# An attention kernel that feeds a mixture of experts: the stage between the two, rebuilt

## The chip, the cores and the metric

The kernel runs on one core of a Trainium2 chip. The metric is the device time of one execution in microseconds (us). The kernel before has a median of 377.03 us over three runs (375.7, 377.03 and 379.55).

## What is computed

The reference has two parts. Attention without softmax, per batch b (8) and head h (8), with 576 rows of 64 numbers:

```python
kv  = einsum('bhsd,bhse->bhde', k, v)
out = einsum('bhsd,bhde->bhse', q, kv)
rms = sqrt(mean(out * out, axis=-1) + 1e-06)
x   = out / rms * g_norm          # then (B,H,S,D) -> (B*S, H*D) = 4608 x 512
```

Then each of the 4608 rows goes to at most one of eight experts:

```python
do_compute = x @ w_skip > 0                 # the other rows stay as they are
logits = xc @ w_gate                        # 8 numbers for each row that is computed
e_idx  = argmax(logits)
gate_w = exp(logits - max)[e_idx] / (sum + 1e-09)
y      = gate_w * (relu(xc @ w1[e_idx]) @ w2[e_idx])    # w1: 512x1024, w2: 1024x512
out    = xc + y
```

## The kernel before

**Attention in units.** The row tiles of attention are worked off as 36 units, numbered n from 0 to 35 (`NU = 36`). A unit is two tiles of 128 rows for half of the heads; two units in a row (u = 0 and 1) make whole rows. The last two units, 34 and 35, take the ninth row of every 64-row group of the last four batches and use small 64x64 products (L504) where the others use 128x128 ones (L496). For a unit, in this order: TensorE turns q (`turn`) and multiplies it with the batch's kv (`values`; its columns also carry 9 more numbers for each head, which add up over the heads to the row's 8 logits and its skip score); ScalarE squares the product (L510); VectorE sums the squares (`squares`, L518); ScalarE takes the root (L525); VectorE inverts it (L532) and multiplies all 584 columns by it (`norm`, L537), which makes `xl`; GpSimd adds up the heads' logits (`finish`, L554 to L562) and multiplies by g_norm (L567), which makes `xb`; SyncE stores `xb` into the output (L602, or L591 for the units of the ninth rows). The product of a unit lies in one of two PSUM buffers `o_ps`, or for units 30 and 33 in `sum_ps`. So the product of unit 35 can start only when `xl` of unit 32 has been read from the buffer.

**The order is written out.** Within `manual_schedule` each engine executes in the order of the program's text. The loop over n (0 to 37) calls the stages of several units, and `at(step, part, job)` hangs further jobs into a step, at its parts "early", "mid", "pe", "dve" and "end".

**From rows to experts.** The rows are ranked in three groups of units (`ends`: 12, 22 and 36 row tiles). For each, `choose` finds the expert of each row on VectorE (six small operations, L614 to L634), `rank` counts on TensorE how many rows of each expert came before (16 small products into the PSUM tile `g_ps`), and `number` makes places of it on VectorE, among them `oha_k`, a table of ones and zeros (L677). `hits` (L690) and `weighed` (L698) make a second table, and `place` (L710) multiplies the two on TensorE, so that each slot of an expert gets its row number. `settle` calls `place` for one part of the row tiles and adds what comes out to `srow` on VectorE (L773).

**Expert 0 starts before attention ends.** Experts are taken in the order of their row counts in the first two groups (22 of the 36 row tiles). From these groups the first 192 slots (`KEPT`) of expert 0 are already known. `early` computes their row numbers and gathers those rows from the output by two indirect DMAs (L863: 128 rows, then 64 rows). `first_in(0)` and `first_in(1)` turn them on TensorE (L801), and ScalarE copies them to `xt_first` (L828, L830). `first_in(0)` also starts the load of expert 0's second weight matrix (`load_second`, L346), which waits for its last transpose. `first_layer_1` computes 2 of the 8 column blocks of layer 1 (`IN = 2`, each 4 products of 192 columns, L814) into a PSUM tile `q_ps`, and ScalarE applies relu (L817). Then attention's pools are closed. Behind them the code at the file's end computes the 6 other blocks (`layer_1`, L1112), the last group's rank and numbers, two calls of `settle`, layer 2 of the 192 rows (`layer_2`, L1124), the row tables (`again_rows`, L1051 on TensorE, and `slot_rows`), and gathers all further rows (L1084). Then `experts` goes through the eight experts. For expert 0, `first_tables` and `again_gates` make the gate weights beside layer 1 of the rest of its rows (148 columns, L1112).

A product of FP32 numbers shows up as two records on TensorE, so 4 products are 8 rows in the trace.

Of the kernel before, what the change touches and what calls it, by code (L numbers as in the profile page):

```python
# [17 lines left out]
def kernel(  # L18
# [148 lines left out]
    def dense(count):  # L167

        for _ in range(count):
            nc.tensor.matmul(out=warm_ps[:, :], lhsT=ones[:, :],  # L170
                             rhs=ones[:, :].unsqueeze(1).to_broadcast([P, 4, P]), start=True, stop=True)
# [311 lines left out]

    def values(n):
        _, b, i, u = units[n]
        qT = qTs.pop(n)

        ps = sum_all if n in THIRDS else \
            ps_o.tile([P, 2, 512], FP32, tag="o", name="o_ps")

        done = turn_8(b, u, ps) if i == 0 else None
        for w in range(2):
            for a in range(2):
                cols = slice(a * KD, (a + 1) * KD)
                if i is not None:
                    nc.tensor.matmul(  # L496
                        out=ps[:, w, 0:2 * PK].rearrange("p (r k) -> p r k", r=2)[:, :, cols],
                        lhsT=qT[:, w, a, :], rhs=kvds[b % KVD][:, u, w, :, cols],
                        start=True, stop=True, skip_group_check=True)
                    continue  # L500
                for hf in range(2):
                    for r in range(2):
                        rows, to = slice(r * 64, (r + 1) * 64), slice(hf * 64, (hf + 1) * 64)
                        nc.tensor.matmul(  # L504
                            out=ps[to, r, w * PK + a * KD:w * PK + (a + 1) * KD],
                            lhsT=qT[rows, w, hf, a * 64:(a + 1) * 64],
                            rhs=kvds[(4 * b + 2 * hf + r) % KVD][rows, u, w, r, cols],
                            start=True, stop=True, skip_group_check=True)
        sq = att_pool.tile([P, 2, 2, 2 * D], FP32, tag="sq", name="sq", bufs=2)
        nc.scalar.activation(out=sq[:, :, :, :], in_=heads(ps, G, G + 2 * D), func=ACT.Square)  # L510
        if done:
            done()
        ops[n] = (ps, sq)
# [14 lines left out]
    def norm(n):  # L528

        nq, b, i, u = units[n]  # L530
        (ps, _), rs = ops.pop(n), rss.pop(n)
        inverse = nc.vector.reciprocal(out=rs[:, :, :], in_=rs[:, :, :])  # L532
        if n < NU - 2:
            scale(n, inverse)
        r4 = rs[:, :, :].unsqueeze(3)
        xl = att_pool.tile([P, 2, 2, PK], FP32, tag="xl", name="xl", bufs=4)
        nc.vector.tensor_tensor(  # L537
            out=xl[:, :, :, :].rearrange("p x y (a k) -> p x (y a) k", a=2),
            in0=ps[:, :, 0:2 * PK].rearrange("p x (h k) -> p x h k", k=KD),
            in1=r4.to_broadcast([P, 2, 4, KD]), op=ALU.mult)  # L540
        return lambda: finish(n, xl)

    def finish(n, xl):
        nq, b, i, u = units[n]
        g = sum(2 * nq >= x for x in ends)
        t0 = 2 * nq - ([0] + ends)[g]
# [9 lines left out]
        if u == 1:  # L556
            del halves[nq]
            nc.gpsimd.tensor_tensor(out=lp[:, 0, :, :, :], in0=lp[:, 0, :, :, :],
                                    in1=lp[:, 1, :, :, :], op=ALU.add)
            both = lp[:, 0, :, :, :] if i is not None else \  # L560
                lp[:, 0, :, :, :].rearrange("p r w g -> p w r g")
            nc.gpsimd.tensor_tensor(out=lgs[g][:, t0:t0 + 2, :], in0=both[:, 0, :, :],  # L562
                                    in1=both[:, 1, :, :], op=ALU.add)
        if u == 0:
# [8 lines left out]
    def scale(n, behind=None):  # L573

        while late:
# [80 lines left out]
    def number(g):  # L656
# [19 lines left out]
        for t in range(0, nt, step):  # L676
            nc.vector.tensor_tensor(out=oha_k[:, t0 + t:t0 + t + step, :],  # L677
                                    in0=row128_i[:, :].unsqueeze(1).to_broadcast([P, step, P]),
                                    in1=lo_i[:, t:t + step].unsqueeze(2).to_broadcast([P, step, P]),
                                    op=ALU.is_equal)  # L680
# [85 lines left out]
    def settle(t0, t1, bv):  # L766
        sp = g_ps[:, GB:GB + 2 * NCOL]
        place(sp, bv, t0, t1 - t0)
        add_pieces(srow[:, :], sp, 2)

# [19 lines left out]
    IN = 2  # L790
# [4 lines left out]
    def first_in(part):  # L795
# [4 lines left out]
        for j in range(DC * m // P):  # L800
            landed = nc.tensor.transpose(out=xp[:, j, :],  # L801
                                         in_=x_of(xg0, off, m)[:, j * P:(j + 1) * P],
                                         identity=ident[:, :])
        turned(xt_first, xp, off, m)
        if part == 0:
            load_second(0, landed)

    def first_layer_1():

        hps = ps_q.tile([P, 512], FP32, tag="q", name="q_ps")  # L810
        for f in range(IN):
            cols = slice(f * KEPT, (f + 1) * KEPT)
            for dc in range(DC):
                nc.tensor.matmul(out=hps[:, cols], lhsT=w_sb[0][0][:, dc, f * P:(f + 1) * P],  # L814
                                 rhs=xt_first[:, dc, :], start=(dc == 0), stop=(dc == DC - 1),
                                 skip_group_check=True)
        at(NU, "early", lambda: nc.scalar.activation(  # L817
            out=ht_first[:, :, :], in_=hps[:, 0:IN * KEPT].rearrange("p (f t) -> p f t", f=IN),
            func=ACT.Relu))
# [20 lines left out]
    NE = ends[LAST - 1]  # L840

    def early():
# [24 lines left out]
        def put():  # L867
            for t in range(NE):
# [76 lines left out]
    now = [0]  # L945
    for part in range(2):
        at(NU - 3 + 2 * part, "early", lambda part=part: first_in(part))
    at(NU - 1, "end", first_layer_1)

    PACE = (2, 4)  # L950
    for n in range(NU + 2):
# [17 lines left out]
        if n == NU:  # L969
            ohc = hits(0, NE, colid_i, gat_pool, NE)  # L970
            drain(choose(LAST))
            scale(NU, chosen[-1])
            first_bv = weighed(ohc, 0, NE, row_k, 2, gat_pool, NE)
# [17 lines left out]
    with tc.tile_pool(name="wpool_b", bufs=1, reuse_waits="tile") as wpool_b, \  # L991
# [375 lines left out]
        def experts(pieces, widths, srcs, xt, ht, yps0, tables, group):  # L1367

            for r in range(E):
# [17 lines left out]
                if r == 0:  # L1387
# [6 lines left out]
                    enter(more[0:1])  # L1394
# [4 lines left out]
                    enter(more[1:])  # L1399
# [69 lines left out]
        layer_1(0, xt_first, ht0, slice(0, KEPT), range(IN, 5))  # L1469
        rank(LAST)  # L1470
        drain(number(LAST))
        layer_1(0, xt_first, ht0, slice(0, KEPT), range(5, FC))
        settle(0, NE, first_bv)
        last_bv = columns(NE, NT - NE, colid_i, row_k, 2, gat_pool, NE)
        y, y_more = [layer_2(0, ht_of, piece, None, range(IN)) for piece in first]
        settle(NE, NT, last_bv)
        layer_2(0, ht_of, first[0], y, range(IN, 3))
        arows = slot_pool.tile([P, NRES], I32, tag="arows", name="arows")
        asrc = slot_pool.tile([P, NRES], I32, tag="asrc", name="asrc")
        again_rows(arows, asrc, range(0, SOON))  # L1480
        rows, src = slot_rows(slice(0, NCOL), slot_pool, "")
        layer_2(0, ht_of, first[0], y, range(3, 4))
        again_rows(arows, asrc, range(SOON, len(runs)))
        layer_2(0, ht_of, first[0], y, range(4, FC))
        for r in range(3):
            gather_all(r, plan, src, asrc)
        gates()
        layer_2(0, ht_of, first[1], y_more, range(IN, 5))
        for piece in plan[0]:
            landed = expert_in(xg0, xt0, piece)  # L1490
        yps0 = [y, layer_2(0, ht_of, first[1], y_more, range(5, FC))]
# [74 lines left out]
```

## Time and profile before

| | us |
|---|---|
| median of three runs | 377.03 (375.7 to 379.55) |
| the profiled execution, its time | 378.6 |
| the profiled execution, its span | 376.7 |
| TensorE matmul busy | 362.9 (96% of the span) |
| VectorE busy | 244.3 (65%) |
| ScalarE busy | 142.9 (38%) |
| GpSimd busy | 122.7 (33%) |
| mean granted TensorE clock | 0.992 |
| products of the last attention unit (n = 35) start | 116.05 |
| layer 1 on the first 192 rows starts | 117.23 |
| layer 1 on expert 0's other rows starts | 144.27 |

A span is the time from the first to the last instruction of the profiled execution; its own time is 1.9 us longer. PE is TensorE, PEld its weight loads, DVE VectorE, ACT ScalarE, POOL GpSimd, SP SyncE. "L537" is line 537 of the kernel before. The granted clock is the share of TensorE's full clock that the chip allowed in a stretch.

### The profile page before, as it was taken

The page shows a single profiled execution, that of the slowest core. Times are in us where ns is not written, and L with a number is a line of the kernel's source. Part 1 is how long each engine was busy: PE and PEld are TensorE (multiplying, and loading weights), DVE is VectorE, ACT ScalarE, POOL GpSimd, SP SyncE. Part 2 cuts the span into 40 slices and gives each one's busy share as a digit, 9 for nine tenths or more (in the row PEclk, how much of TensorE's full clock was granted, in tenths as well). Part 3 has the DMA queues.
Part 4 walks back from the last instruction along what each step waited for, and adds up shares of the span by engine and source line. Part 5 has one row for each costly group of instructions (what it writes and reads, how often), then busy time and mean ns, then how long its engine had stood idle before and what let it go on. Part 6 is the DMA issues. An engine that isn't in the chain of part 4 may idle for free.

```text
span 376.7 us, 9624 instructions
## 1 busy us (share of the span) xinstructions
PE 362.9 (96%) x3848; PEld 314.8 (84%) x3848; DVE 244.3 (65%) x626; ACT 142.9 (38%) x383; POOL 122.7 (33%) x195
## 2 busy tenths in 40 slices
PE   8899999999988999999999999999999999999994
PEld 4687897898977948779979987988998998998983
DVE  3355367767787763566766675876876776878831
ACT  2466576666773212214402430430440430431420
POOL 7035467655668435323013302202302302102003
PEclk9999999999998999999999999999999999999998
DMA  8999999996487718967427362671762762700001
GB/s 289 395 391 391 401 405 396 405 384 206 132 302 213 232 39 281 392 237 252 168 98 222 114 225 76 239 244 46 284 197 72 274 209 80 269 3 28 30 1 53
DMA packets 32039, 81.70 MB, mean 217 GB/s; under 512 B 2474, under 2 KB 2482, under 8 KB 31988
## 3 DMA queue, kind: packets, MB, share of 16 engines
q1 hardware_dynamic: 28176, 69.47, 52.0%
q0 software_dynamic: 3792, 11.53, 9.2%
q8 instruction: 32, 0.52, 0.6%
q14 instruction: 19, 0.16, 0.1%
q10 hardware_dynamic: 20, 0.02, 0.0%
HBM read 66.80 MB, written 14.48 MB: 216 GB/s over the span
## 4 chain that ended last, share of the span: by engine, by line
PE 82%; issue 6%; DMA 3%; ACT 3%; DVE 3%; POOL 2%; SPq 0%; POOLq 0%; DVEq 0%; ACTq 0%
PE bank L1192 44%; PE bank L1124 9%; PE o_ps L496 6%; PE sum_ps L379 4%; PE bank L1112 4%; PE q_ps L460 3%; PE g_ps L393 2%; DMA v<-in_v_dram 2%; PE bank L1093 2%; PE q_ps L814 1%; DMA xg<-out_dram,src 1%; DVE rs L518 1%; DVE xl L537 1%; ACT sq L510 1%; PE g_ps L411 1%
## 5 line engine op out<-in xcount | busy, mean ns | idle before, releaser
L1202 ACT COPY p<-bank 128x128 f32<-128x128 f32 (+6 forms) x70 | 20.8, 297 | 99.2 <-PE bank L1192 88.5
L1192 PE MATMUL bank<-xt,w 128*128 128x128 f32 (+5 forms) x336 | 55.4, 288 | 0.0
L567 POOL TENSOR_TENSOR xb<-xl,g_b 128x512 f32<-128x512 f32 x36 | 43.5, 1211 | 32.5 <-DVE rs L532 30.6
L1323 POOL DMA_INDIRECT out_dram<-xg,rows x14 | 14.4, 1027 | 120.8 <-DVE xg L1320 117.6
L1192 PEld LDWEIGHTS bank<-xt,w 128*128 128x128 f32 x336 | 47.0, 190 | 1.9 <-DVE bank L1196 1.4
L1196 DVE TENSOR_TENSOR bank<-bank,p 128x128 f32<-128x128 f32 (+6 forms) x70 | 23.6, 337 | 30.2 <-PE bank L1192 29.1
L496 PE MATMUL o_ps<-kvd,qT 128*128 128x146 f32 x240 | 35.8, 290 | 1.0 <-ACT kvd L415 0.7
L1192 PE MATMUL bank<-xs,s 128*128 128x128 f32 (+5 forms) x224 | 36.7, 289 | 0.0
L518 DVE TENSOR_REDUCE rs<-sq 128x8 f32<-128x512 f32 x36 | 24.6, 682 | 15.3 <-ACT sq L510 15.1
L496 PEld LDWEIGHTS o_ps<-kvd,qT 128*128 128x128 f32 x240 | 31.6, 188 | 2.0 <-ACT kvd L415 1.5
L1124 PE MATMUL bank<-w,ht 128*32 128x128 f32 (+2 forms) x436 | 33.2, 318 | 0.0
L1192 PEld LDWEIGHTS bank<-xs,s 128*128 128x128 f32 x224 | 31.1, 190 | 1.0 <-ACT p L1202 0.8
L537 DVE TENSOR_TENSOR xl<-o_ps,rs 128x584 f32<-128x584 f32 x34 | 26.1, 767 | 4.5 <-DVE rs L532 0.5
L1124 PEld LDWEIGHTS bank<-w,ht 128*32 128x32 f32 (+2 forms) x436 | 19.3, 120 | 11.6 <-issue 8.3
L1192 PE MATMUL bank<-t,ht 128*128 128x256 f32 x112 | 27.0, 384 | 0.0
L1192 PE MATMUL bank<-w,ht 128*128 128x256 f32 x112 | 26.5, 380 | 0.0
L510 ACT ACTIVATE sq<-o_ps 128x512 f32<-128x512 f32 x34 | 20.3, 597 | 15.0 <-PE o_ps L496 14.4
L379 PE MATMUL sum_ps<-v,k 64*64 64x64 f32 x1152 | 24.7, 223 | 0.8 <-issue 0.6
L1192 PE MATMUL bank<-t,hs 128*128 128x256 f32 x112 | 25.3, 379 | 0.0
L379 PEld LDWEIGHTS sum_ps<-v,k 64*64 64x64 f32 x1152 | 20.9, 134 | 4.7 <-issue 1.7
L1084 POOL DMA_INDIRECT xg<-out_dram,src x14 | 13.8, 985 | 33.3 <-DMA out_dram<-xg,rows 17.3
L1192 PEld LDWEIGHTS bank<-t,ht 128*128 128x128 f32 x112 | 20.8, 190 | 3.9 <-issue 1.2
(217 smaller groups left out, 671.0 us busy)
## 6 DMA issues: line engine op xcount, KB each, us to landing
w<-in_moe_w_dram SPq DMA_DIRECT2D x16, 2048.0 KB, 10.0
k<-in_k_dram SPq DMA_DIRECT2D x16, 576.0 KB, 9.1
v<-in_v_dram SPq DMA_DIRECT2D x16, 576.0 KB, 11.0
q<-in_q_dram SPq DMA_DIRECT2D x16, 576.0 KB, 10.5
out_dram<-xb SPq DMA_DIRECT2D x29, 256.0 KB, 8.0
out_dram<-xb POOLq DMA_DIRECT2D x7, 256.0 KB, 6.4
xg<-out_dram,src POOLq DMA_INDIRECT x16, 3.5
out_dram<-xg,rows POOLq DMA_INDIRECT x16, 6.0
```

What stands on the lines that cost most here:

```text
L379: nc.tensor.matmul(out=sum_ps[w * 64:(w + 1) * 64, a, u, :], lhsT=kt[r, 2 * u + w, c, :], rhs=vt[r, 2 * u + w, c, :], start=(c == 0), stop ...
L496: nc.tensor.matmul(out=ps[:, w, 0:2 * PK].rearrange("p (r k) -> p r k", r=2)[:, :, cols], lhsT=qT[:, w, a, :], rhs=kvds[b % KVD][:, u, w, ...
L510: nc.scalar.activation(out=sq[:, :, :, :], in_=heads(ps, G, G + 2 * D), func=ACT.Square)
L518: nc.vector.tensor_reduce(out=rs[:, :, :], in_=sq[:, :, :, :].rearrange("p x y (a d) -> p x (y a) d", a=2), axis=AX.X, op=ALU.add)
L537: nc.vector.tensor_tensor(out=xl[:, :, :, :].rearrange("p x y (a k) -> p x (y a) k", a=2), in0=ps[:, :, 0:2 * PK].rearrange("p x (h k) -> ...
L567: late.append((lambda: nc.gpsimd.tensor_tensor(out=xb[:, :, 4 * u * D:(4 * u + 4) * D].rearrange("p r (w x) -> p r w x", w=2), in0=xl[:, : ...
L1112: nc.tensor.matmul(out=hps[:, cols], lhsT=w_sb[r][0][:, dc, f * P:(f + 1) * P], rhs=xt[:, dc, cols], start=(dc == 0), stop=(dc == DC - 1))
L1124: nc.tensor.matmul(out=yps[q * m:(q + 1) * m, 0:n], lhsT=ht(f)[:, off:off + m], rhs=w_sb[r][1][:, f, q * n:(q + 1) * n], start=(f == 0), s ...
L1192: nc.tensor.matmul(out=out, lhsT=lhsT(i), rhs=rhs(i), start=start and i == 0, stop=i == k - 1, skip_group_check=True)
L1196: nc.vector.tensor_tensor(out=to, in0=x, in1=y, op=ALU.add)
L1202: nc.scalar.copy(out=t, in_=x)
L1323: ins = nc.gpsimd.indirect_dma_start(out=cut_rows(m)[:, :], out_offset=bass.IndirectOffsetOnAxis(ap=rows[:, col:col + 1], axis=0), in_=x, ...
```

## The change

- `IN` goes from 2 to 4: half of layer 1 of the first 192 rows is computed inside the attention loop. The first block is split: its first 128 columns come ahead of the products of unit 35, its other 64 and the three further blocks come behind them. Blocks 0 and 1 go into the tile `g_ps`, blocks 2 and 3 into `q_ps`.
- Three products of constants (`dense(3)`, 128x512 in bf16) are put at the start of step 33. `first_in(0)` moves from the start of step 33 to behind that step's attention products, and `first_in(1)` from the start of step 35 to behind the products of unit 34.
- The load of w2 of expert 0 no longer waits for the first rows' last transpose but for the products of unit 32.
- For the last two units, VectorE no longer makes `xl`. It multiplies only the logits' columns (`last_logits`, 4 operations) and adds all of them up in one reduction; GpSimd's four additions go. ScalarE makes the 64 columns of each head in `norm_by_scalar`, 8 activations for each unit. The relu of blocks 0 and 1 comes behind the eight of unit 34, that of blocks 2 and 3 behind the eight of unit 35.
- `rank` and `number` of the last group follow at once, ahead of the rest of layer 1. The two sums of `settle` become one: both `place` calls add into one PSUM tile and `srow` is updated once. The table of the known rows (`hits`) is made one step earlier. The last `xb` waits for the last operation of `number`.
- In `early`, one multiplication for `xb` on GpSimd is put ahead of the first gather.
- Behind attention the order becomes: place the first 22 tiles, blocks 4 and 5, layer 2 on blocks 0 to 3 for the first 128 rows, place the last 14, layer 2 on the same blocks for the other 64 rows, row tables, blocks 6 and 7, gathers, the rest of layer 2. The row tables move to another pool (`gat_pool`).
- For expert 0, two pieces of the next expert's rows are turned ahead of `again_gates`, where it was one.

```diff
-    IN = 2
+    IN = 4
...
-        if part == 0:
-            load_second(0, landed)
-
-    def first_layer_1():
-
-        hps = ps_q.tile([P, 512], FP32, tag="q", name="q_ps")
-        for f in range(IN):
-            cols = slice(f * KEPT, (f + 1) * KEPT)
+
+    first_ps = [g_ps[:, 0:2 * KEPT]]
+
+    def first_layer_1(fs, cols):
+
+        for f in fs:
+            hps = first_ps[f // 2][:, f % 2 * KEPT:(f % 2 + 1) * KEPT]
...
+    def first_hidden(pair):
+        nc.scalar.activation(
+            out=ht_first[:, 2 * pair:2 * pair + 2, :],
+            in_=first_ps[pair].rearrange("p (f t) -> p f t", f=2), func=ACT.Relu)
+
+    def first_rest():
+
+        first_ps.append(ps_q.tile([P, 512], FP32, tag="q", name="q_ps")[:, 0:2 * KEPT])
+        first_layer_1(range(1), slice(P, KEPT))
+        first_layer_1(range(1, IN), slice(0, KEPT))
...
     for part in range(2):
-        at(NU - 3 + 2 * part, "early", lambda part=part: first_in(part))
-    at(NU - 1, "end", first_layer_1)
+        at(NU - 3 + part, "pe", lambda part=part: first_in(part))
+    at(NU - 4, "pe", lambda: load_second(0, valued[-1]))
+    at(NU - 3, "early", lambda: dense(3, ps_q.tile([P, 512], FP32, tag="q", name="q_ps")))
+    at(NU - 1, "early", lambda: first_layer_1(range(1), slice(0, P)))
+    at(NU - 1, "mid", lambda: known_at.append(hits(0, NE, colid_i, gat_pool, NE)))
+    at(NU - 1, "end", first_rest)
...
+        if n >= NU - 2:
+            last_logits(n, ps, rs)
+            last_x.append(lambda: norm_by_scalar(n, ps, rs, xl))
+            return None
...
+    def last_logits(n, ps, rs):
...
+        for a in range(2):
+            nc.vector.tensor_tensor(
+                out=le[:, :, :, 4 * u + a:4 * u + a + 3:2].rearrange("p r g w -> p r w g"),
+                in0=ends_of(heads(ps, 0, PK))[:, :, :, a, :],
+                in1=rs[:, :, a:a + 3:2].unsqueeze(3).to_broadcast([P, 2, 2, G]), op=ALU.mult)
+        if u == 1:
+            g, t0 = place_of_logits(nq)
+            nc.vector.tensor_reduce(out=lgs[g][:, t0:t0 + 2, :], in_=halves.pop(nq)[:, :, :, :],
+                                    axis=AX.X, op=ALU.add)
+
+    def norm_by_scalar(n, ps, rs, xl):
+
+        for r in range(2):
+            for h in range(4):
+                w, a = divmod(h, 2)
+                cols = slice(G + a * D, G + (a + 1) * D)
+                nc.scalar.activation(out=xl[:, r, w, cols],
+                                     in_=heads(ps, cols.start, cols.stop)[:, r, w, :],
+                                     func=ACT.Copy, scale=rs[:, r, h:h + 1])
+        weigh(n, xl)
...
         def put():
+            scale(now[0])
...
         if n == NU:
-            ohc = hits(0, NE, colid_i, gat_pool, NE)
+            for pair, job in enumerate(last_x):
+                job()
+                first_hidden(pair)
             drain(choose(LAST))
-            scale(NU, chosen[-1])
-            first_bv = weighed(ohc, 0, NE, row_k, 2, gat_pool, NE)
+            scale(NU, chosen[-1], 1)
+            first_bv = weighed(known_at[0], 0, NE, row_k, 2, gat_pool, NE)
+            rank(LAST)
+            drain(number(LAST))
+            scale(NU, counted[-1])
...
-                    enter(more[0:1])
+                    enter(more[0:2])
...
-                    enter(more[1:])
+                    enter(more[2:])
...
-        layer_1(0, xt_first, ht0, slice(0, KEPT), range(IN, 5))
-        rank(LAST)
-        drain(number(LAST))
-        layer_1(0, xt_first, ht0, slice(0, KEPT), range(5, FC))
-        settle(0, NE, first_bv)
+        sp = g_ps[:, GB:GB + 2 * NCOL]
+        place(sp, first_bv, 0, NE, True, False)
         last_bv = columns(NE, NT - NE, colid_i, row_k, 2, gat_pool, NE)
-        y, y_more = [layer_2(0, ht_of, piece, None, range(IN)) for piece in first]
-        settle(NE, NT, last_bv)
-        layer_2(0, ht_of, first[0], y, range(IN, 3))
+        first_1(range(IN, 6))
+        y = layer_2(0, ht_of, first[0], None, range(IN))
+        place(sp, last_bv, NE, NT - NE, False, True)
+        add_pieces(srow[:, :], sp, 2)
+        y_more = layer_2(0, ht_of, first[1], None, range(IN))
...
         again_rows(arows, asrc, range(0, SOON))
-        rows, src = slot_rows(slice(0, NCOL), slot_pool, "")
-        layer_2(0, ht_of, first[0], y, range(3, 4))
+        rows, src = slot_rows(slice(0, NCOL), gat_pool, "")
+        first_1(range(6, 7))
         again_rows(arows, asrc, range(SOON, len(runs)))
-        layer_2(0, ht_of, first[0], y, range(4, FC))
+        first_1(range(7, FC))
         for r in range(3):
             gather_all(r, plan, src, asrc)
+        layer_2(0, ht_of, first[0], y, range(IN, FC))
         gates()
-        layer_2(0, ht_of, first[1], y_more, range(IN, 5))
         for piece in plan[0]:
             landed = expert_in(xg0, xt0, piece)
-        yps0 = [y, layer_2(0, ht_of, first[1], y_more, range(5, FC))]
+        yps0 = [y, layer_2(0, ht_of, first[1], y_more, range(IN, FC))]
```

## The prediction

> **What bounds the kernel now.** I read the page's chain of waits first:
>
> ```profile
> PE 82%; issue 6%; DMA 3%; ACT 3%; DVE 3%; POOL 2%; SPq 0%; POOLq 0%; DVEq 0%; ACTq 0%
> ```
>
> TensorE carries the end, so an edit is worth what it takes from TensorE's own time, by idle time removed or products made faster. The second view, what TensorE waited for between 100 and 160 us, lists every idle stretch that this change can reach:
>
> ```profile
> PE o_ps L504 <- DVE xl L537: 1.4, 1, 1.4
> PE q_ps L801 <- DMA xg<-out_dram,src: 1.1, 1, 1.1
> PE q_ps L814 <- ACT xt_first L830: 0.4, 1, 0.4
> PE g_ps L879 <- DVE rows L873: 0.3, 1, 0.3
> PE g_ps L1051 <- DVE gate L773: 0.2, 1, 0.2
> ```
>
> Only 3.4 us in all: filling waits is worth 3 us at most. The third view is TensorE's timeline there (start, duration, records):
>
> ```profile
> 111.94 0.63 PE L801 MATMUL q_ps<-ident,xg 128*128 128x128 f32 x4 [1.10 <-DMA xg<-out_dram,src]
> 112.40 1.17 PE L496 MATMUL sum_ps<-kvd,qT 128*128 128x146 f32 x8
> 113.57 0.74 PE L504 MATMUL o_ps<-kvd,q 64*64 64x73 f32 x32
> 114.25 0.44 PE L801 MATMUL q_ps<-ident,xg 128*128 128x128 f32 x2
> 116.05 0.74 PE L504 MATMUL o_ps<-kvd,q 64*64 64x73 f32 x32 [1.36 <-DVE xl L537]
> 117.23 4.55 PE L814 MATMUL q_ps<-xt_first,w 128*128 128x192 f32 x16 [0.44 <-ACT xt_first L830]
> 121.61 4.06 PE L1112 MATMUL bank<-xt_first,w 128*128 128x192 f32 x24
> ```
>
> The last two lines have the same product shape, yet 16 records took 4.38 us to the next line's start and 24 took 4.06. At L1112's 0.169 us, 16 records are 2.71; 1.67 us are lost with no wait. The fourth view, busy time by stretch, says why (after the five engines comes the granted clock):
>
> ```profile
> 117.20:118.00 0.80, 0.77 (x5) 0.77 (x6) 0.68 (x2) 0.48 (x1) 0.80 (x2) 1.00 0.94 282
> 118.00:118.50 0.50, 0.50 (x4) 0.50 (x4) 0.50 (x2) 0.07 (x1) 0.50 (x2) 0.66 1.01 254
> 120.00:121.00 1.00, 1.00 (x4) 1.00 (x4) 1.00 (x2) 0.00 (x0) 0.86 (x3) 0.50 1.14 319
> 121.50:122.00 0.50, 0.50 (x5) 0.50 (x4) 0.18 (x1) 0.18 (x1) 0.22 (x1) 0.93 0.81 238
> ```
>
> The clock is halved from about 118.17 (0.34 of the second row at half) to 121.57: 3.4 us, half of it lost, 1.7 us, the same sum. Behind 122 the stretch to the end has clock 1.00 and is busy for 248.9 of 254.7 us, so time won ahead of it should reach the end.
>
> **Part by part: TensorE up to the last attention unit.** In step 33 the turning of the first rows waited for the gather (landed at 111.81) with the unit's products behind it. The change puts those first; they need `xl` of unit 30 out of `sum_ps` (L537, 111.09 + 0.77 = 111.86), so they start at 111.9, not 112.40. ScalarE's square and VectorE's sums come 0.5 earlier, and `xl` of unit 32 ends near 115.5, not 116.0. The three constant products lie in the idle time from 110.85 to 111.9 (they wait for `q_ps`, read by 111.11); their like, the 512-column records at 0.43 us for FP32, bound them at 1.3 us above; nearer is half, as they are bf16: 0.2 each, 0.65 in all. Above that bound they would push 0.5 us; I take zero. Turning then runs 113.05 to 113.65, unit 34's products to 114.4, the second turning (its buffer is free with the copy to `xt_first`, near 114.35) to 114.85, the first 128 columns of block 0 (8 records at 0.137, as L801) to 115.95, and unit 35's products to 116.7. That fills the 1.36 us wait, but the last unit ends only 0.1 us sooner.
>
> **Behind it.** The 0.44 us wait for `xt_first` goes (copied by 115.8). Block 0's other 64 columns are bounded by half of 1.1 us below and 1.1 above: L402's 36 columns still take 0.135 a record, so 1.1. Block 0 cost 1.35, so 0.25 is won. Blocks 1 to 3 take 3 x 1.35 and end at 121.8 at full clock.
>
> **The clock.** The Trainium skill, "TensorE: Matmul & The Clock Gate", section "Why this matters for your kernels", asks for no idle gaps over about 3 us. By that rule gaps of 1.10, 1.36 and 0.44 could not have closed the gate, and constants or fill would change nothing: the change would be worth 0.6. By the row, the clock fell after a stretch (114.7 to 118.1) with 1.8 us idle and 0.74 us of small 64x64 products, not one long gap. I follow the row: filling takes the idle out of just this stretch and 1.7 us come back. The page's other statement, a free-running window of about 3.4 us, agrees with the measured length; it would also mean that another execution can have the fall elsewhere or not at all.
>
> **The chain to rank.** L537's two last operations (0.77 each) leave VectorE; four of 128x36 (L773's 0.18 to 0.2 each) and a reduction of 0.27 come. The `hits` operation (0.70) now stands ahead of unit 35's sum and holds it by 0.45. So: `xl` of unit 33 ends at 117.1, `hits` 117.8, sum 118.5, root (ScalarE) 118.8, logits 119.8. Before, GpSimd's four additions gave them at 121.78 (L562). The six steps of `choose` take 1.65 (121.81 to 123.45 before): ready at 121.4. `rank` also waits for relu of blocks 0 and 1, since both use `g_ps`, and that stands on ScalarE behind eight activations. The rows:
>
> ```profile
> L1202 ACT COPY p<-bank 128x128 f32<-128x128 f32 x16 | 4.3, 266 | 20.5 <-PE bank L1192 19.9
> L1114 ACT ACTIVATE ht<-bank 128x192 f32<-128x192 f32 x6 | 2.0, 332 | 6.4 <-PE bank L1112 6.4
> L525 ACT ACTIVATE rs<-rs,eps_t 128x8 f32<-128x8 f32 x36 | 10.9, 303 | 4.2 <-DVE rs L518 4.1
> ```
>
> 64 columns lie below 0.27 by the first; L525, the one with a per-row operand as here, needs 0.30 for 8 columns. "ScalarE: Activation LUTs", section "Rules for kernel authors", gives 0.3 us and 0.83 ns per element, 0.35 here as an estimate. I take 0.30: 118.8 + 8 x 0.30 + 0.49 (relu, L817) = 121.7, just ahead of TensorE at 121.8; by the page's 0.35 it is 122.1 and costs 0.3. Relu of blocks 2 and 3 follows at 124.6, needed near 128. GpSimd's `xb` of unit 34 waits for ScalarE at 121.2, but its queue has unit 33's to 122.6 anyway.
>
> **A new wait.** `rank` (0.85) is now followed on TensorE by `place`, which overwrites what `number`'s first two operations read (0.28 + 0.16, L662, L663), and needs `weighed` (1.25, done by 122.7). Before, three blocks of layer 1 stood between. TensorE idles 0.45, and all of layer 1 and 2 is queued behind it. `oha_k` (2.1) is ready near 126 for the last 14 tiles, due near 130: hidden by blocks 4 and 5 and 3.4 us of layer 2. Without that cover it would cost 2.5.
>
> **Queues.** Unit 35's `xb` waits for `number` (126), its two stores leave SP near 127.5 instead of 128.04; gathers want them at 134 rather than 137. The load of w2 passes a store on SP (held by GpSimd until 113.6) and starts near 111 rather than 114.44, beside the second gather, which it used to follow. In `early` an `xb` (1.19) on GpSimd precedes the first gather, in a 1.91 us idle stretch ending at 107.98; without the idle time it would delay the gather by 1.2. The exponentials (1.28 + 0.45) move behind relu of block 7, to 138.5; their table is due at 146. One sum fewer on VectorE and the row tables' other pool: off the path, zero. The second turned piece ahead of `again_gates` covers the 0.2 wait in L1051: 0.2 won.
>
> Sum: 0.1 + 0.44 + 0.25 + 1.67 + 0.2 - 0.45 = 2.2, say 2.3 with the smaller joints. The profiled span 376.7 becomes 374.4, its time of 378.6 becomes 376.3. That execution lies 1.6 above the median of 377.03; applied to the median: **374.7**.
>
> **Rivals.**
> *The clock is not won* (0.20): it falls in the new kernel too, in the stall behind `rank` or elsewhere, or ordinary executions of before do not have it. For: the window's phase is free, and utilisation, not a gap, decides. Against: the new stretch has no idle over 0.5. Worth 0.6: 376.4.
> *The fill is cheaper than its rows* (0.25): 64 columns at half the price (0.5), the stall behind `rank` covered (0.45), earlier gathers relieve joints (0.2). 2.3 + 1.15 = 3.4: 373.6.
> *w2 on top of the second gather* (0.07), the one that ends slower. The first gather landed in 3.8 us beside w1's tail; the slowest indirect transfer in this stage took 9.0. Issued near 110.3, the second may land at 119.3 where its turning is due at 114.4; unit 35's products and all of layer 1 stand behind it. 4.9 lost against 2.3: 379.6. It decides from a landing time of 6.4 us. Against: the gather is small and issued before w2.
> *As summed* (0.48).
>
> **Numbers.** One per cent, 3.8 us, is about what a measurement of this kernel tells from no change (its runs span 375.7 to 379.55). The range, 372.6 to 377.6, holds the first, second and last case with 0.5 to 1 us for a median's scatter and leaves the slow case out. Faster by over 1% (below 373.3): half of the cheap-fill case and over a quarter of the main one, because a median of before near the four executions' mean (377.7) adds 0.7: 0.30. Slower by over 1%: the third rival's tail, 0.06. Within: 0.64.
>
> **What would show it.** Right: granted clock 1.00 from 111 to 125; products of unit 35 ending near 116.7; logits near 120; an idle of about 0.45 between `rank` and `place`; the first 148-column product of layer 1 near 142.2 instead of 144.27. Wrong: TensorE waiting for the second gather, for ScalarE's relu ahead of `rank`, or for the stores ahead of the gathers; or a clock of 0.5 elsewhere.

## The result, and the profile after

The changed kernel takes 375.67 us (median of ten runs, 375.25 to 376.79). The kernel before, beside it, took 378.14 (median of ten, 375.7 to 379.55), 1.1 us more than the median of its first three. The ratio on record, which is not simply that of the two medians, is 0.9943, with a 95% interval of 0.9922 to 0.9964: two microseconds, under one per cent. The profiled execution has a span of 374.4 us and a time of 376.26.

The chain of waits of the changed kernel:

```profile
PE 83%; issue 6%; POOL 4%; DVE 3%; ACT 3%; POOLq 0%; DVEq 0%; ACTq 0%
```

TensorE still carries the end. What TensorE waited for between 100 and 160 us (total, times, longest, all in us):

```profile
PE g_ps L759 <- DVE top L711: 0.8, 1, 0.8
PE g_ps L931 <- DVE rows L925: 0.3, 1, 0.3
PE q_ps L170 <- ACT qT L463: 0.3, 1, 0.3
```

Five waits became three. Those for the first rows, for `xl`, for `xt_first` and for `gate` are gone; the one for `rows` stays, and 0.3 us are left ahead of the constants (L170); the new one stands where it was forecast, at the first `place`, and is nearly twice as long. TensorE's timeline there (start, duration, records):

```profile
110.28 1.17 PE L498 MATMUL o_ps<-kvd,qT 128*128 128x146 f32 x8
111.75 0.81 PE L170 MATMUL q_ps<-ones 128*128 128x512 bf16 x3 [0.31 <-ACT qT L463]
...
116.21 0.74 PE L508 MATMUL o_ps<-kvd,q 64*64 64x73 f32 x32
116.88 2.46 PE L856 MATMUL g_ps<-xt_first,w 128*128 128x64 f32 x16
119.18 2.76 PE L856 MATMUL q_ps<-xt_first,w 128*128 128x192 f32 x16
121.79 0.48 PE L693 MATMUL g_ps<-top,ident 128*128 128x120 f32 x2
...
123.71 0.71 PE L759 MATMUL g_ps<-bv,oha_k 128*128 128x48 bf16 x22 [0.79 <-DVE top L711]
...
142.31 4.29 PE L1173 MATMUL bank<-xt,w 128*128 128x148 f32 x32
```

The row at 119.18 has 16 records in 2.61 us to the next row. The same 16 records took 4.38 in the profile before. The stretches show the clock (the 1.00 or less behind the five engines):

```profile
115.00:118.00 3.00, 3.00 (x51) 2.80 (x52) 2.73 (x7) 1.95 (x5) 2.84 (x6) 1.00 0.92 311
118.00:122.00 4.00, 4.00 (x25) 3.85 (x25) 3.44 (x15) 2.69 (x13) 2.33 (x5) 1.00 1.00 385
122.00:126.00 4.00, 3.21 (x50) 2.97 (x50) 3.97 (x8) 1.91 (x9) 3.28 (x2) 1.00 0.27 86
```

No fall here. So the two profiles seem to confirm the forecast nearly line by line: the clock restored, the idle time ahead of `place`, layer 1 of 148 columns at 142.31 (forecast 142.2), the span of 374.4 exactly. Two questions remain. Was the clock restored by the change, or would another execution of the kernel before have had it as well? And which parts of the change earn the rest?

**A measure for the stage.** The start of the profiled execution, up to the first products of attention, differs from run to run by more than the effect looked for (the first record into `o_ps` starts between 16.07 and 17.71 us in ten of the profiles, of both kernels and of variants). So the stage is measured from the start of unit 32's products (109.68 before, 110.28 after) to the first product of 148 columns, and from there to the first of 172 columns, in the next expert (163.38 after). In us:

| kernel | to 148 | on to 172 | clock at 104 to 130 |
|---|---|---|---|
| before | 34.59 | 21.37 | falls at 118 |
| before, again (e5) | 32.85 | 21.37 | 1.00 |
| before, constants added (e1) | 33.84 | 22.29 | 1.00 |
| after | 32.03 | 21.07 | 1.00 |
| after, again (e6; e12) | 32.06; 32.03 | 21.07; 21.07 | 1.00 |
| no constants (e2) | 32.08 | 21.90 | 1.00 |
| no fill (e3) | 32.03 | 22.06 | 1.00 |
| neither (e7) | 32.07 | 21.07 | 1.00 |
| old last logits (e8; e10) | 33.51; 35.19 | 21.07; 21.07 | 1.00; falls at 125 |
| old logits and constants (e9) | 33.53 | 21.07 | 1.00 |
| place later (e4; e11) | 31.42; 31.44 | 22.11; 21.07 | 1.00 |

Where no fall and no stall comes in between, these repeat to 0.05 us, far better than whole times do. The 0.8 to 1.0 us by which e1 to e4 exceed the others behind the 148 columns go with a stall of TensorE between 146 and 149 us that the trace puts down to nothing ("issue"; 0.4 to 0.9 us of it are listed); in e1 0.7 us of such a stall lie right ahead of them, too, in the 1.0 us that it has over e5. These stalls are in all profiles of that chip and in none of the others.

### The profile page after: what moved, and what is told of

Its sections match the earlier page's. It is cut to its first block, busy times and chain, and to the rows that moved or that the text cites. A ratio compares the mean times of both kernels' runs of the same rounds, so it can differ in the third digit from the quotient of the medians.

```text
span 374.4 us, 9661 instructions
## 1 busy us (share of the span) xinstructions
PE 363.2 (97%) x3859; PEld 315.2 (84%) x3859; DVE 244.3 (65%) x627; ACT 146.0 (39%) x398; POOL 123.1 (33%) x191
## 4 chain that ended last, share of the span: by engine, by line
PE 83%; issue 6%; POOL 4%; DVE 3%; ACT 3%; POOLq 0%; DVEq 0%; ACTq 0%
PE bank L1253 44%; PE bank L1185 9%; PE o_ps L498 7%; PE sum_ps L379 5%; PE bank L1173 4%; PE q_ps L460 3%; PE g_ps L393 2%; PE q_ps L170 2%; PE bank L1154 2%; POOL xb L615 2%; DVE xl L545 1%; DVE rs L522 1%; PE g_ps L411 1%; ACT qT L463 1%; ACT sq L514 1%
## 5 line engine op out<-in xcount | busy, mean ns | idle before, releaser
L1185 PE MATMUL bank<-w,ht 128*32 128x128 f32 (+2 forms) x424 | 29.9, 313 | 0.0
L545 DVE TENSOR_TENSOR xl<-o_ps,rs 128x584 f32<-128x584 f32 x32 | 24.5, 767 | 4.3 <-DVE rs L536 0.5
L1185 PEld LDWEIGHTS bank<-w,ht 128*32 128x32 f32 (+2 forms) x424 | 18.2, 119 | 10.7 <-issue 7.6
L1145 POOL DMA_INDIRECT xg<-out_dram,src x14 | 15.6, 1116 | 33.3 <-DMA out_dram<-xg,rows 18.0
```

The source lines that it names most:

```text
L545: nc.vector.tensor_tensor(out=xl[:, :, :, :].rearrange("p x y (a k) -> p x (y a) k", a=2), in0=ps[:, :, 0:2 * PK].rearrange("p x (h k) -> ...
L1145: nc.gpsimd.indirect_dma_start(out=x_of(xg, off, m), out_offset=None, in_=cut_rows(m)[:, :], in_offset=bass.IndirectOffsetOnAxis(ap=idx[:, ...
L1185: nc.tensor.matmul(out=yps[q * m:(q + 1) * m, 0:n], lhsT=ht(f)[:, off:off + m], rhs=w_sb[r][1][:, f, q * n:(q + 1) * n], start=(f == 0), s ...
```

## The experiments

All kernels compute the whole reference; none leaves work out. Those on the same chip are told together.

**Was it the constants and the fill?** (e1 to e3.) First, the constants alone put into the kernel before, into its longest wait:

```diff
-    def dense(count):
+    def dense(count, ps=warm_ps):
...
-            nc.tensor.matmul(out=warm_ps[:, :], lhsT=ones[:, :],
+            nc.tensor.matmul(out=ps[:, :], lhsT=ones[:, :],
...
+    at(NU - 1, "early", lambda: dense(6, g_ps))
```

> The kernel before, with nothing moved; six constant products of 512 columns are put into the 1.36 us wait ahead of unit 35's products. Theory (most of the gain is the clock, which fell because this stretch had little work in it): the granted clock stays at 1.00 from 117 to 122, the 16 records of layer 1 behind unit 35 take 2.7 us instead of 4.4, and the time falls by 1.2 to 1.7 us on average. Rival (the gain is useful work put into the waits, and the fall of the clock is not caused by them): the clock falls as before, and the time is within 0.3 us of before.

Measured: 379.33 us against 379.41 for the kernel before on that chip, ratio 0.9988 (0.9972 to 1.0004). Its profile has full clock, and block 0 and 1 take 2.70 us:

```profile
118.00:122.00 4.00, 3.78 (x23) 3.78 (x24) 3.62 (x7) 1.46 (x4) 3.53 (x8) 1.00 0.99 294
```

But the median does not move. If every execution of the kernel before lost 1.67 us there, it would have. What does change is the tail: a mean granted clock under 0.9935 came in 7 of 19 executions of before on this chip and in 1 of 14 with the constants, and the means differ by 0.5 us. That is too few runs to show it, but it is what a fall in a part of the executions would look like.

Then the kernel after without its constants:

```diff
-    at(NU - 3, "early", lambda: dense(3, ps_q.tile([P, 512], FP32, tag="q", name="q_ps")))
```

> The changed kernel without the three constant products. Theory: the other fill suffices for the clock (1.00 from 111 to 125) and the products hid in idle time, so the time is within 0.4 us of the changed kernel. Rival (the constants hold the clock up): the clock falls to 0.5 for 3.4 us somewhere between 112 and 122 and 1.5 us are lost against the changed kernel.

Measured: 377.14, ratio 0.9927 (0.9902 to 0.9953); clock 1.00, a wait of 1.1 us for `xl` in the place of the constants, and the stage unchanged. And without the fill, all of block 0 behind unit 35:

```diff
-    at(NU - 1, "early", lambda: first_layer_1(range(1), slice(0, P)))
...
-        first_layer_1(range(1), slice(P, KEPT))
-        first_layer_1(range(1, IN), slice(0, KEPT))
+        first_layer_1(range(IN), slice(0, KEPT))
```

> The changed kernel with all of block 0 behind unit 35's products, as one piece of 192 columns, so that the wait for the buffer of unit 32 is empty again. Theory: the idle of about 1.2 us returns ahead of unit 35 and the clock falls behind it as in the kernel before: 0.3 us for the work that is no longer done early, plus up to 1.7 us for the clock, 1 to 2 us slower than the changed kernel. Rival (filling is only work moved): 0.3 us slower or less, clock at 1.00.

Measured: 377.74, ratio 0.9944 (0.9922 to 0.9965), clock 1.00, and this in TensorE's waits:

```profile
PE o_ps L508 <- DVE xl L545: 0.8, 1, 0.8
PE g_ps L759 <- DVE top L711: 0.7, 1, 0.7
```

The wait for `xl` is back, and yet the stage takes the same 32.03 us. The split costs what the wait saves: four blocks unsplit take 5.31 us, split 5.90. What is left over only lengthens the wait at `place`, because that waits for VectorE. Both parts are worth nothing in these profiles, in time or in clock. (The kernel after was not on this chip; its ratio on others is 0.993 to 0.995.)

**Is the new wait worth its place?** (e4.) Blocks 4 and 5 are put ahead of the first `place`:

```diff
+        first_1(range(IN, 6))
         place(sp, first_bv, 0, NE, True, False)
         last_bv = columns(NE, NT - NE, colid_i, row_k, 2, gat_pool, NE)
-        first_1(range(IN, 6))
```

> The changed kernel with the placing of the first 22 tiles put behind blocks 4 and 5 of layer 1. Theory: the 0.79 us wait between rank and place is filled by these blocks, and 0.6 to 0.8 us are won against the changed kernel, less up to 0.2 because VectorE's table for the last 14 tiles is then due sooner. Rival (that wait hides another one, such as ScalarE's or the table's): within 0.2 us of the changed kernel, with a wait of 0.5 us or more at another place.

Measured: 376.62, ratio 0.9925 (0.9904 to 0.9946). The wait is gone, nothing is late in its stead, and the stage takes 31.42 instead of 32.03: 0.6 us won, of the 0.8 that were idle. The kernel after was not on this chip, so the same is done once more below.

**Does the clock of before fall in each execution?** (e5 to e7, another chip.) The kernel before itself:

> The kernel before, profiled once more. Theory: the clock falls to 0.5 for about 3.4 us again, at a place within 2 us of 118, since the stretch ahead of it (1.8 us idle, small products) is the same. Rival (the fall was an accident of the one execution): clock 1.00 from 110 to 125, and the 16 records of layer 1 behind unit 35 take 2.7 us.

Measured: 377.76 (378.16 over all its runs on that chip). Its profile has all the idle time, and the clock does not fall behind it. In its timeline, and then in its stretches:

```profile
117.13 0.74 PE L504 MATMUL o_ps<-kvd,q 64*64 64x73 f32 x32 [1.31 <-DVE xl L537]
118.31 2.87 PE L814 MATMUL q_ps<-xt_first,w 128*128 128x192 f32 x16 [0.44 <-ACT xt_first L830]
121.02 4.06 PE L1112 MATMUL bank<-xt_first,w 128*128 128x192 f32 x24
```

```profile
10.00:11.00 1.00, 1.00 (x4) 0.25 (x2) 0.90 (x9) 0.00 (x0) 0.00 (x0) 0.50 1.06 394
118.00:122.00 4.00, 3.69 (x23) 3.69 (x24) 3.62 (x7) 1.55 (x5) 3.75 (x8) 1.00 0.99 302
```

16 records took 2.71 us, with waits of 1.03, 1.31 and 0.44 ahead of them, practically those of the first profile. This execution has a fall at its start instead (0.50 at 10 us). So the fall at 118 belongs to some executions only. Without it the stage takes 32.85 us, and the change wins 0.82 up to the 148 columns and 0.30 behind them: 1.12 us. Beside it, the kernel after:

> The changed kernel itself, on the chip of the next two, so that they can be set against it. Both theories: ratio to before within 0.992 to 0.997, clock 1.00 from 110 to 125, a wait of 0.8 us between rank and place.

Measured: 375.82, ratio 0.9929 (0.9902 to 0.9957), stage as in its first profile. And the kernel after with neither fill nor constants (both diffs above):

> The changed kernel with neither the constant products nor the 128 columns ahead of unit 35: idle again about 1.1 us ahead of step 33's products and 0.8 us ahead of unit 35's. Theory (idle in this stretch lets the clock fall): 0.5 for 3.4 us, 1 to 1.7 us slower than the changed kernel. Rival (what is left, 1.9 us idle in two pieces within 6 us, is too little, and the fall needs the full idle and late turning of the kernel before): clock 1.00 and within 0.4 us of the changed kernel.

Measured: 376.03, ratio 0.9934 (0.9907 to 0.996). It waits for 1.1 and 0.8 us where the two parts stood and for 0.7 at `place`; the clock is 1.00 through the whole stage, and the stage takes 32.07. The stretch in which the clock of before fell:

```profile
118.00:122.00 4.00, 4.00 (x27) 4.00 (x26) 3.54 (x13) 2.38 (x11) 3.06 (x6) 1.00 0.95 335
```

The two parts do nothing together either.

**Is it the early logits?** (e8.) The kernel after, with VectorE's `xl` and GpSimd's four additions back for the last two units:

```diff
-        if n >= NU - 2:
-            last_logits(n, ps, rs)
-            last_x.append(lambda: norm_by_scalar(n, ps, rs, xl))
-            return None
...
-            for pair, job in enumerate(last_x):
-                job()
+            for pair in range(2):
                 first_hidden(pair)
```

> The changed kernel with the last two units as before: VectorE makes all columns (two operations of 0.77 us), GpSimd adds the logits. Theory (this part brings the logits forward by about 1.5 us, and rank, now ahead of the rest of layer 1, depends on it): rank waits for choose, layer 1's rest with it, and 1.2 to 1.8 us are lost against the changed kernel. Rival (the wait between rank and place is set by VectorE's other work and has room): less than 0.5 us lost.

Measured: 378.48, ratio 1.0018 (0.9998 to 1.0037): the whole gain is lost, and more. Its waits:

```profile
PE g_ps L692 <- DVE ohb L678: 1.6, 1, 1.6
PE g_ps L755 <- DVE top L707: 0.8, 1, 0.8
```

`rank` stands ahead of half of layer 1 now, so late logits leave TensorE idle for 1.6 us. That is 1.45 in the stage (33.51 against 32.06 on the same chip); the medians of after and of this kernel differ by 2.7. The other 1.2 us are in no line of this profile. 11 of its 14 executions had a mean clock under 0.9935, which suggested a fall that the profiled one did not have.

**Does that idle time bring the clock down?** (e9 to e12, a third chip.) The same kernel, and eight constant products in the 1.6 us:

```diff
                 first_hidden(pair)
             drain(choose(LAST))
...
             first_bv = weighed(known_at[0], 0, NE, row_k, 2, gat_pool, NE)
+            dense(8, sum_all[:, 0, :])
             rank(LAST)
```

> The kernel after with the old way for the logits of the last two units (as in the earlier run of that kind, which took 378.5 us, 2.7 more than after on its chip, of which its profiled stage explains 1.45), and eight constant products of about 0.21 us put into the 1.6 us that TensorE waits there ahead of rank. Theory (the rest of those 2.7, about 1.2 us, are clock falls that follow from the 2.4 us of idle time around rank): the run without constants on this chip is about 1.2 us slower than this one, ratio to before near 0.9985 instead of 1.002. Rival (constants do nothing, the falls have another cause or the rest is another stall): both within 0.3 us of each other.

> The kernel after with the old logits, without constants, once more, beside the one with them. Theory: ratio to before near 1.002, mean granted clock below 0.993 in most executions; if the profiled execution has a fall, it lies between 120 and 130 us, the busy share of TensorE there being well below one. Rival: the same time as with constants, and the fall at the start of the span or nowhere.

Measured: 377.69 (ratio 0.9988, 0.9969 to 1.0007) with the constants, 378.3 (1.001, 0.9992 to 1.0028) without; the means differ by 0.9. The two profiles are a pair as clean as one can wish. With constants, then without, from TensorE's timeline:

```profile
120.94 1.89 PE L170 MATMUL sum_ps<-ones 128*128 128x512 bf16 x8
122.67 0.38 PE L689 MATMUL g_ps<-top,ident 128*128 128x120 f32 x2
122.93 0.21 PE L692 MATMUL g_ps<-ohb,ut 128*128 128x112 bf16 x1
...
124.91 2.85 PE L1169 MATMUL bank<-xt_first,w 128*128 128x192 f32 x16
127.59 3.60 PE L1181 MATMUL bank<-w,xg 128*128 128x512 f32 x8
```

```profile
120.94 0.38 PE L689 MATMUL g_ps<-top,ident 128*128 128x120 f32 x2
122.93 0.21 PE L692 MATMUL g_ps<-ohb,ut 128*128 128x112 bf16 x1 [1.61 <-DVE ohb L678]
...
124.36 0.71 PE L755 MATMUL g_ps<-bv,oha_k 128*128 128x48 bf16 x22 [0.79 <-DVE top L707]
124.91 4.53 PE L1168 MATMUL bank<-xt_first,w 128*128 128x192 f32 x16
129.28 3.60 PE L1180 MATMUL bank<-w,xg 128*128 128x512 f32 x8
```

Both are at the same work at 122.93 and at 124.91, to the hundredth; the constants hid in the wait and cost nothing. Then the same 16 records take 2.68 us in one and 4.37 in the other. The stretches of the one without constants say why:

```profile
124.50:125.00 0.50, 0.50 (x23) 0.50 (x21) 0.47 (x2) 0.00 (x0) 0.50 (x1) 1.00 0.00 0
125.00:126.00 1.00, 1.00 (x7) 1.00 (x5) 1.00 (x3) 0.00 (x0) 1.00 (x2) 0.63 0.07 16
126.00:127.00 1.00, 1.00 (x5) 1.00 (x5) 1.00 (x1) 0.00 (x0) 0.23 (x1) 0.50 0.82 188
128.50:129.00 0.50, 0.50 (x4) 0.50 (x4) 0.40 (x2) 0.00 (x0) 0.50 (x1) 0.83 0.51 115
```

Half clock from 125.26 to 128.67: 3.4 us again, 1.7 of them lost; the spans are 375.0 and 376.7. Over all executions, a mean clock under 0.9935 came in 1 of 14 with the constants and in 13 of 20 without. So constants do keep the clock up, where idle time of this size stands; and a fall does not come in each execution. The expected 1.2 us were too many for the medians (0.6 apart), since falls come in part of the runs: if each low mean clock stands for one such fall, 13 of 20 against 1 of 14 at 1.7 us each are 1.0 us on the mean, and 0.9 was measured.

On the same chip, the place experiment with its comparison:

> The kernel after with layer 1's blocks 4 and 5 ahead of the first place, once more, now beside the kernel after on the same chip. Theory: the idle 0.8 us ahead of place goes, nothing is late in its stead, and 0.6 us are won: ratio to before 0.0016 lower than after's. Rival (blocks 4 and 5 then wait for the same VectorE work elsewhere, or the second place becomes late): within 0.2 us of after.

> The kernel after itself, as the measure for the three others. Theory: ratio to before 0.993 to 0.995, the profiled stage from the products of unit 32 to the first 172-column product 53.1 us. Rival: none; it is the comparison.

Measured: 375.02 (ratio 0.9931, 0.9911 to 0.9951) against 376.26 for the kernel after (0.9949, 0.9931 to 0.9968). From TensorE's timeline with `place` later:

```profile
121.39 0.59 PE L699 MATMUL g_ps<-ohb,ones 128*128 128x112 bf16 x14
121.84 2.85 PE L1173 MATMUL bank<-xt_first,w 128*128 128x192 f32 x16
124.52 0.72 PE L759 MATMUL g_ps<-bv,oha_k 128*128 128x48 bf16 x22
...
128.83 0.51 PE L759 MATMUL g_ps<-bv,oha_k 128*128 128x48 bf16 x14
```

Neither `place` waits. The stage takes 31.44 instead of 32.03, as on the other chip; by the ratios it is 0.7 us, by the medians 1.2, and the intervals overlap. The 0.6 us of the trace are shown twice, once on each of two chips. This version has the lowest median of all on this chip.

## Why the prediction was right, and where not

The forecast was 374.7 us, with a range of 372.6 to 377.6; 375.67 lies in it, and the change stays within the one per cent that the prediction put down as most likely. The sum that led to it was 2.3, and the two profiled spans differ by 2.3. Inside the sum, however, the terms are not what they were taken for.

**The clock: 1.67 counted, in part of the executions only.** The step that failed is "I follow the row: filling takes the idle out of just this stretch and 1.7 us come back". The 1.7 us were rightly measured in one execution, and wrongly carried over to the median. In the traces of before it is there once (34.59) and missing once (32.85). How often it comes can't be read directly, since a mean clock also counts falls elsewhere, at the start (as in e5 and e12, near 8 to 12 us) and in the last 3.5 us of the span; on the third chip 25 of 46 executions of before were under 0.9935, and 2 of 13 of after. If it came in about one in two, it would be worth 0.9 us on the mean; since an execution with its fall at the start (e5) has the same mean clock of 0.992, that is an upper estimate. The first rival had named this ("ordinary executions of before do not have it"), with a chance of 0.20; as a thing that holds in half of the runs it should have been part of the main case.

The reason was half wrong too. The fill and the constants were to keep the clock, but without both (e7) it stays up in the profiled execution, with 1.1 and 0.8 us idle in that stretch, and 5 of its 6 executions have a mean clock of 0.996. What the runs leave: no fall in the stage in eight profiles of the kernel after or near it, with 0.3 to 2.6 us idle in pieces of up to 1.1, spread over 12 us; one in two with 1.6 and 0.8 close together (e8, e10); one in two with 1.1, 1.3 and 0.4 and small products (before, e5).

Over all their executions a mean clock under 0.9935 came in 13 of 63 for these eight (e3 and e4 with two of six each), and in 48 of 92 for before: rarer, but not gone, and where in the span it fell is known for the profiled ones alone. That idle time close together counts fits all the profiles: the most that any 3.4 us of this stage hold is 1.8 us in before and 2.4 in e8 and e10, where falls came, and 1.3 or less in the others (1.29 in e1, the wait for the first rows). The longest single gap would fit, too, but only with a limit between the 1.29 of e1 and the 1.31 of e5; no run tells the two apart. That filling the longer of two gaps keeps the clock is shown by e9. Where the limit lies is open.

On the rule of the Trainium skill, "TensorE: Matmul & The Clock Gate", section "Why this matters for your kernels", against the row: no gap ahead of the two falls was over 1.61 us, and the clock fell nonetheless, so the row was the right guide to what can happen, and a single row no guide to how often.

**The rest: 0.54 forecast, 1.12 measured without a fall.** By the trace of before without a fall (e5) against that of after, summed over the stage, row start to row start:

| term | us |
|---|---|
| idle time, 3.01 to 1.10 | -1.91 |
| three constant products | +0.70 |
| layer 1 of the first rows, 10.60 to 11.34 | +0.74 |
| `rank`, 0.71 to 1.13 | +0.42 |
| layer 2 of the first rows, 11.41 to 10.52 | -0.89 |
| the rest | -0.18 |
| sum | -1.12 |

- "say 2.3 with the smaller joints" put at 0.1 what is 0.89: layer 2 of these rows is now in four pieces of code, where it was in seven, with as many products. Two records alone took 1.04 us to the next row's start in e5, and eight in a row took 3.43, 0.43 each, in after (e5 first):

```profile
133.45 1.10 PE L1124 MATMUL bank<-w,ht 128*128 128x512 f32 x2
134.49 0.28 PE L1051 MATMUL g_ps<-srow,ident 128*64 128x1 f32 x4
```

```profile
126.95 3.60 PE L1185 MATMUL bank<-w,xg 128*128 128x512 f32 x8
130.38 0.51 PE L759 MATMUL g_ps<-bv,oha_k 128*128 128x48 bf16 x14
```

  That each change of piece had cost some 0.3 (0.89 over three) is argued, not tested: no run has the new order of layer 2 alone. This is the term that was overlooked.
- The new wait was put at 0.45 and measured 0.79. Counted from unit 32, the logits came as forecast (10.08 us; forecast 10.12), while TensorE had its blocks done 0.6 earlier (11.51; forecast 12.12) and waits for the same VectorE chain. Of `rank`'s 0.42, 0.28 are such a wait, too, though no view lists it: its second row starts at 122.28, when VectorE has ended `ohb` (121.96 + 0.27); in e7, where TensorE came later, the first row passes in 0.21 instead of 0.49. And `choose` began 0.15 late, held by GpSimd's logits of units 32 and 33 (L605). `weighed` (1.25) stands there between `ohb` and the two operations that `place` waits for:

```profile
120.06 0.30 DVE L573 TENSOR_REDUCE lg<-le 128x18 f32<-128x144 f32 x1
120.51 0.27 DVE L662 TENSOR_REDUCE mx<-lg 128x14 f32<-128x112 f32 x1 [0.15 <-POOL lg L605]
...
122.15 1.25 DVE L747 TENSOR_TENSOR bv<-ohc,row_k 128x1056 bf16<-128x1056 bf16 x1
123.32 0.27 DVE L710 TENSOR_TENSOR pr<-g_ps,ohb 128x112 f32<-128x112 f32 x1
123.50 0.15 DVE L711 COPY top<-g_ps 128x8 f32<-128x8 f32 x1
```

  So here the VectorE chain from logits to `top`, not TensorE's work, sets when `place` can start. That is why the fill is worth nothing, why 1.5 us later logits cost 1.45, and why blocks moved ahead of `place` (e4, e11) fill its wait.
- The 0.44 wait for `xt_first` and the 0.2 in `again_gates` are gone, as forecast. The part behind the 148 columns is 0.30 shorter.
- ScalarE: `relu` of blocks 0 and 1 starts at 121.20, ahead of TensorE, and nothing waits for it. An activation of 64 columns took 0.22 in sequence (the eight take 1.75), not the 0.30 of the nearest row, nor the 0.35 that was estimated by the rule of "ScalarE: Activation LUTs", section "Rules for kernel authors", in the Trainium skill:

```profile
119.61 1.75 ACT L582 ACTIVATE xl<-o_ps,rs 128x64 f32<-128x64 f32 x8 [0.30 <-DVE rs L536]
121.20 0.54 ACT L861 ACTIVATE xg<-g_ps 128x384 f32<-128x384 f32 x1
```

- `oha_k` was taken at 2.1 and took 3.03, and the second `bv` 1.65 instead of 0.86. GpSimd was multiplying `xb` beside a part of each (two of these took 3.28 us instead of 2.4); that this made them longer is argued from the overlap, not tested. The cover held: `place` of the last 14 tiles did not wait.
- The stores of unit 35 left at 129.02, not 127.5, since unit 35's `xb` waits for `number`, and so for `oha_k`. No product waited for a gather.
- The rival that ends slower (w2 on top of the second gather) did not happen. w2 left at 111.58, the turning of the second piece ran at 114.95, and the indirect transfers landed in 3.3 us at the median.

**The number.** 374.7 was 2.3 below the median of three runs of before. That median was itself 1.1 below the later one of ten, and this makes up the 1.0 by which the forecast lay under 375.67. The match of the span is partly luck: the execution after came to unit 32 0.6 us later, and its stage was 2.86 shorter (2.56 and 0.30), of which 1.7 were the fall of the execution before.

By the ratios of three comparisons the change wins 1.9 to 2.7 us. The stage gives 1.1 of it, shown by traces (one of before without a fall, three of after). The falls, at one in two, would give up to 0.9; that is an estimate, and the listed clocks speak for less. Among executions of 0.9935 and above, before and after still differ by 1.5 us on the third chip (377.45 for 21, 375.95 for 11) and by 2.1 beside e6 (377.41 for 11, 375.33 for only 3). So 0.4 to 1.0 us are accounted for neither by the stage nor by this split. They do not lie behind the stage: from the first 172 columns to the end, the profiles of before, e5, after, e6 and e12 all take 211.0 to 211.1 us.

## What to carry to other kernels

A clock fall in one profile can be a chance event with a price (here 1.7 us), not a fixed cost: before it is counted as a gain, take a second profile of the same kernel, and weigh the fall by how often it comes. Filling a wait is worth something only if the engine that is filled is the one that the next joint waits for; here the next joint waited for VectorE's chain, so fill and constants were passengers. The early logits are needed by the new order: without them its whole gain is lost. But they are not all of it. In e7, with neither fill nor constants, 0.88 of the 1.08 us won on e5 are the shorter layer 2 of the first rows. Neither the early logits nor the new order of layer 2 was put into the kernel before by itself, so what each is worth alone is open. Measure a stage between two products in the trace: apart from falls and stalls it repeats to 0.05 us, where whole times scatter by 3.

## What the runs showed of the hardware

- The granted clock fell to a half for 3.4 us in two places with no idle stretch over 1.61 us ahead of it, and in an execution of the same kernel with the same waits it did not.
- The first 16 to 18 us vary by up to 1.6 us between executions of kernels that do the same work there; in three profiles (e5, e6, e12) the clock is at a half for some 3.4 us between 7 and 12 us.
- On one chip of those used, all four profiles show a stall of TensorE between 146 and 149 us (0.4 to 0.9 us listed, and 0.8 to 1.0 longer to the next expert) that nothing in the trace explains, and the kernel before takes 379.4 there, against 378.1 on the others.
- The same layer 2 products of the first rows took 11.41 us in seven pieces (e5) and 10.52 in four (after), without a wait listed between them.
